# Reversing copies in eight parts, silu in single pieces and a weight gradient by column halves

## The chip, the core and the metric

The kernel runs on one core of one Trainium2 chip. The metric is the device time of one execution in microseconds (us). The core has a matrix engine (TensorE, PE in the profile; its weight loads are shown as PEld), a vector engine (VectorE, DVE), an engine for activation functions and copies (ScalarE, ACT), a general engine (GpSimd, POOL) and a queue engine (SyncE, SP). SP, ACT and POOL issue DMA transfers. Each engine takes its own instructions in a fixed order; semaphores join the engines.

## The reference

The program computes the output of a block and all its gradients. Of 2048 tokens and 576 channels, `A_u` is normalized; a state-space convolution `s` (a kernel from 128 complex rates for each channel, applied over the sequence) is gated by a feed-forward network with 4608 hidden columns.

```python
def _B_ref(x, w1, w3, w2):
    gate = jnp.einsum("bsd,df->bsf", x, w1)
    up = jnp.einsum("bsd,df->bsf", x, w3)
    h = _silu(gate) * up
    out = jnp.einsum("bsf,fd->bsd", h, w2)
    return out
...
    xn = _layernorm(x, axis=-1)
    s = _A_ref(xn, A_A_re, A_A_im, A_B_re, A_B_im, A_C_re, A_C_im, A_log_dt, A_Dskip)
    g = _silu(_B_ref(xn, B_w1, B_w3, B_w2))
    return x + s * g
...
    _out, _vjp = jax.vjp(_f, A_u, A_A_re, A_A_im, A_B_re, A_B_im, A_C_re, A_C_im, A_log_dt, A_Dskip, B_w1, B_w3, B_w2)
    _grads = _vjp(grad_out)
    _out0 = jnp.asarray(_out)
    return (_out0, *[jnp.asarray(_g) for _g in _grads])
```

`out_0` is the output, `out_1` the gradient of `A_u`, `out_2` to `out_9` those of the convolution's parameters, and `out_10`, `out_11` and `out_12` those of `w1`, `w3` and `w2`.

## The kernel before

The 2048 tokens are 16 tiles of 128 rows. The odd tiles are handled with their rows reversed, since the Fourier transforms work with sums and differences of mirrored rows. So `A_u` and `grad_out` are copied in DRAM, with the rows of each odd tile reversed, to a scratch tensor `odd`, and `out_0` and `out_1` are written for the odd tiles to `odd` and then copied back, reversed. The function `turned` gives the view of the eight odd tiles with their rows in reverse. A row has 1152 bytes, a whole copy 1152 KB.

The stages, in order of time. (1) Normalization, the state-space kernel and the gate and up products of the network (`ffn_hidden`, 72 steps of two tiles by 512 hidden columns). POOL stores the gate and up values (`G_dram`, `U_dram`), SP the hidden values. (2) `ffn_output`: w2's product for each tile, the output, and `go_o`, the gradient at the network's output. (3) The gradient groups: 18 groups of 256 hidden columns, with the gradient of the convolution in four quarters beside groups 0 to 10, and the sums for the state-space parameters (`param_step`) from group 11 on. (4) `phase6_inputs`: the gradient of `A_u`, tile by tile, odd tiles first, with the rest of the parameter sums beside it.

One gradient group `gi` runs through these stages (`phase6_group`, `phase6_grad13`). In "h0" to "h3" PE multiplies the output gradient with w2 into PSUM tiles `ph` (line 1746, 20 matmuls of 256 columns for a stage), ACT copies them to `gh` (line 1749), and DVE multiplies `gh` into the prepared tiles `gu` and `gg` (line 1764). "stored" is the store of both to DRAM on SP. Then come nine blocks of weight gradients: four 128-row blocks for `out_11`, four for `out_10` (line 1807, 16 matmuls each, copied by ACT at line 1809) and a tail of 32 matmuls for the last 64 rows of both (lines 1817 and 1819). They use two PSUM buffers, `pgw`, in turn. w2's own gradient (`phase6_grad2`, line 1787, 32 matmuls of 288 columns for 128 hidden columns) is called at "h1" and "h3" and takes both buffers at once, one for each half of the 576 output columns; ACT copies them at line 1791.

`phase6_prep` prepares the next group: silu of the gate values into `gu` (line 1713), the derivative of silu into `gg` (line 1717), and on DVE the products of both with the up values (lines 1720 and 1721). It is a generator; the loop in `backward` calls `next(prep)` at chosen stages, and each call emits the work up to the next `yield`. Each of silu and its derivative is done in four quarters of the tokens, in two calls of two quarters. The calls are at "h2" and "h3" for silu, at the first two blocks of `out_11` for the derivative, and at the next four blocks for one quarter of the products each.

What sets the order: `issue_after` puts an instruction behind another on its engine, and `self.sc` chains the ACT copies and activations of the groups in the order in which the program emits them. `self.at` gives a planned time; a planner orders what isn't chained by these times and by when inputs are ready.

The reversing copies before: `grad_out` in one copy on ACT's queue during the state-space kernel (line 569); `out_0` in one copy on SP at the start of the gradient groups (line 1200); `out_1` in two copies of four tiles each on POOL (line 1934), emitted at the 11th and 14th tile of the last stage and issued by the planner as soon as their inputs are stored.

## Time and profile before

| | |
|---|---|
| median of 3 runs | 1788.87 us (1781.19 to 1794.86) |
| the profiled execution | 1793.5 us |
| its span | 1791.7 us |
| granted clock of TensorE, mean | 0.988 |
| HBM read and written | 135.60 and 190.89 MB |

The span is the time from the first instruction to the last; the page divides it among the engines. A row of the waits names the instruction that stood still, what released it, the total time, the number of times and the longest. A row of a timeline gives start and duration in us, engine, line, what is written and read, how many instructions are merged, and in square brackets how long the engine was idle before and what ended that. SPq is the sequencer of SP, which issues transfers in order. A row of the groups gives the number of instructions, their busy time in us, the mean of one in ns, and the idle time before them.

### The profile page before, as it was taken

What the parts mean: (1) busy time and instruction counts of PE and PEld (TensorE: products, weight loads), DVE (VectorE), ACT (ScalarE), POOL (GpSimd) and SP (SyncE); (2) the same over time, 40 slices, a digit from 0 to 9 for tenths busy, and PEclk for the clock granted to TensorE, in tenths of its full rate; (3) what the DMA queues carried; (4) which work ended last, traced back from release to release, by engine and by line L of the source; (5) the groups of instructions that cost most, each with busy time, mean ns of one, the idle gap of its engine ahead of it and who ended that gap; (6) DMA issues with size and microseconds to landing.
All of it is one profiled execution on the core that took longest, in us unless ns stands there. A gap on an engine that the chain in (4) does not pass through costs nothing. (4 is left out here: it accounts for less than half of the span.)

```text
span 1791.7 us, 38769 instructions
## 1 busy us (share of the span) xinstructions
PE 1664.5 (93%) x15637; PEld 1228.2 (69%) x15637; DVE 1358.6 (76%) x2102; ACT 912.5 (51%) x1649; POOL 347.1 (19%) x565
## 2 busy tenths in 40 slices
PE   7789999999999999989999999999999987989997
PEld 3455555554545777777888888888888765768875
DVE  8768888887692555858978889659999955858675
ACT  6778888886864112764666666564445410101001
POOL 3112222213134111101111111111111233131032
PEclk9999999999999999999999999999999999999999
DMA  7789999889698989748666756589999999999992
GB/s 225 266 271 343 321 343 316 297 271 275 212 294 245 233 195 196 219 145 238 190 179 206 202 174 191 158 221 275 247 262 241 220 232 235 211 212 225 233 240 48
DMA packets 635483, 416.90 MB, mean 233 GB/s; under 512 B 424407, under 2 KB 575943, under 8 KB 630695
## 3 DMA queue, kind: packets, MB, share of 16 engines
q1 hardware_dynamic: 579620, 287.34, 64.5%
q0 software_dynamic: 31904, 106.81, 18.2%
q10 hardware_dynamic: 23778, 20.28, 4.2%
q8 instruction: 122, 2.00, 0.5%
q14 instruction: 59, 0.48, 0.1%
HBM read 135.60 MB, written 190.89 MB: 182 GB/s over the span
## 5 line engine op out<-in xcount | busy, mean ns | idle before, releaser
L1857 PEld LDWEIGHTS <-acts 128*128 128x128 bf16 x2304 | 224.9, 98 | 75.2 <-DMA acts<-GU_dram 11.4
L1807 PEld LDWEIGHTS <-xn_bf 128*128 128x128 bf16 x2304 | 224.5, 98 | 44.6 <-issue 18.4
L1394 DVE TENSOR_TENSOR pr_q<-et_ps,pz 128x1024 f32<-128x1024 f32 x144 | 176.0, 1222 | 29.5 <-PE et_ps L1389 14.8
L1857 PE MATMUL px<-wT,acts 128*128 128x288 bf16 x1472 | 191.6, 288 | 1.5 <-DMA wT<-in_B_w_dram 1.5
L1746 PE MATMUL ph<-w2T,goT 128*128 128x256 bf16 x1440 | 176.2, 275 | 8.7 <-ACT gh L1749 8.5
L1025 PEld LDWEIGHTS <-xnT 128*128 128x128 bf16 x1152 | 107.0, 98 | 109.2 <-issue 18.3
L1397 DVE TENSOR_REDUCE S_all<-pr_q 128x32 f32<-128x1024 f32 x144 | 175.3, 1217 | 3.1
L1746 PEld LDWEIGHTS <-goT 128*128 128x128 bf16 x1440 | 140.4, 99 | 28.8 <-issue 11.4
L1025 PE MATMUL pg<-wmB_w,xnT 128*128 128x512 bf16 x576 | 154.0, 380 | 2.1 <-ACT g_t L1041 1.8
L1025 PE MATMUL pu<-wmB_w,xnT 128*128 128x512 bf16 x576 | 154.3, 379 | 0.0
L1787 PE MATMUL pgw<-go_o,h_n 128*128 128x288 bf16 x1152 | 149.0, 286 | 0.2
L1807 PE MATMUL pgw<-gu_n,xn_bf 128*128 128x256 bf16 x1152 | 135.2, 273 | 10.4 <-ACT gw L1791 5.5
L1787 PEld LDWEIGHTS <-h_n 128*128 128x128 bf16 x1152 | 112.3, 98 | 30.0 <-issue 2.0
L1807 PE MATMUL pgw<-gg_n,xn_bf 128*128 128x256 bf16 x1152 | 130.5, 272 | 2.4 <-ACT gw L1809 2.3
L1809 ACT CAST gw<-pgw 128x256 bf16<-128x256 f32 x144 | 52.3, 374 | 144.6 <-PE pgw L1807 144.5
L1039 ACT ACTIVATE s_t<-pg 128x512 bf16<-128x512 f32 x144 | 87.8, 610 | 74.0 <-PE pu L1033 36.2
L1857 PE MATMUL px<-wA,acts 128*128 128x288 bf16 x832 | 110.5, 288 | 15.7 <-DMA acts<-GU_dram 10.5
L674 ACT ACTIVATE cs_k<-et_ps 128x512 bf16<-128x512 int16 x216 | 111.5, 630 | 0.1
L1749 ACT CAST gh<-ph 128x512 bf16<-128x512 f32 x144 | 81.3, 600 | 54.9 <-PE ph L1746 54.9
L1913 ACT ACTIVATE go<-gx 128x576 bf16<-128x576 f32 x16 | 10.9, 684 | 193.1 <-DVE gx L1896 109.4
L1053 POOL DMA_DIRECT2D G_dram<-g_t x72 | 52.4, 727 | 285.0 <-DVE g_t L1043 146.4
L1044 ACT CAST u_t<-pu 128x512 bf16<-128x512 f32 x144 | 87.4, 607 | 7.6 <-PE pu L1025 7.5
(316 smaller groups left out, 3206.0 us busy)
## 6 DMA issues: line engine op xcount, KB each, us to landing
U_dram<-u_t POOLq DMA_DIRECT2D x72, 256.0 KB, 5.3
G_dram<-g_t POOLq DMA_DIRECT2D x72, 256.0 KB, 4.7
H_dram<-h_t SPq DMA_DIRECT2D x72, 256.0 KB, 4.0
Q_dram<-q_k SPq DMA_DIRECT2D x36, 512.0 KB, 4.7
gg_n<-G_dram POOLq DMA_DIRECT2D x18, 1024.0 KB, 6.7
h_n<-U_dram POOLq DMA_DIRECT2D x18, 1024.0 KB, 8.6
GU_dram<-gu_n SPq DMA_DIRECT2D x36, 512.0 KB, 4.3
GG_dram<-gg_n SPq DMA_DIRECT2D x36, 512.0 KB, 10.5
```

The lines of the kernel that those rows point to most:

```text
L674: self.sin_last = nc.scalar.activation(out=CS[:, :, o:o + 256], in_=pt[:].bitcast(I16)[:, :, 0::2], func=ACT.Sin, scale=6.283184 / 2 ** 16)
L1025: ins = nc.tensor.matmul(pt[:], lhsT=xnT[:, c, ts], rhs=wm[w][:, c, :], start=(q == 0 and c == 0), stop=(q == 1 and c == nfull - 1))
L1039: nc.scalar.activation(out=s_t[:, :, q, :], in_=pgv, func=ACT.Silu)
L1044: nc.scalar.copy(out=u_t[:, :, q, :], in_=puv)
L1053: self.u_stores[step] = nc.gpsimd.dma_start(out=dst[fb * ng:(fb + 1) * ng, :, i0:i0 + NT, :].rearrange("g p t f -> p g (t f)"), in_=src[:] ...
L1394: nc.vector.tensor_tensor(out=pr[:].rearrange("p r k e -> p r (k e)"), in0=T[h][:].rearrange("p k z d a -> p (k z d a)")[:, None].to_broad ...
L1397: nc.vector.tensor_reduce(out=self.S_all[:, :, d0:d0 + 4], in_=pr[:].rearrange("p r k (d a) -> p (r k) d a", d=4), op=ALU.add, axis=AX.X)
L1746: self.pe_last = nc.tensor.matmul(ph[j][:, k, :].rearrange("p (a f) -> p a f", f=P), lhsT=lw, rhs=rh, start=(n == 0), stop=(n == nfull))
L1749: self.sc(lambda: nc.scalar.copy(out=gh[:, j], in_=ph[j][:]))
L1787: self.pe_last = nc.tensor.matmul(pgw[pi_][:, 0:pw], lhsT=hn[:, tt, fl * P:(fl + 1) * P], rhs=go_o[:, tt, po:po + pw], start=(tt == 0), st ...
L1807: self.pe_last = nc.tensor.matmul(pw_[:, 0:FG], lhsT=self.xn_bf[:, tt, c * P:(c + 1) * P], rhs=nat[:, tt, :], start=(tt == 0), stop=(tt == ...
L1857: self.pe_last = nc.tensor.matmul(px[pi_][:, 0:pw], lhsT=acts[i][:, ai, fi, :], rhs=w[:, po:po + pw], start=(n == 0), stop=(n == len(steps ...
```

## The change

1. `grad_out`: instead of one copy on ACT's queue, eight pieces of 16 row positions of each odd tile on POOL's queue, each behind the store of a step (36 to 50, every second one) of `ffn_hidden`.
2. `out_0`: instead of one copy on SP, eight pieces on SP, one in each of groups 2 to 9, behind the group's last store to `GG_dram` (`turn_out`).
3. `out_1`: instead of two copies of four whole odd tiles, eight pieces of 16 row positions of all eight odd tiles on POOL, two emitted at each of the 11th to 14th tile.
4. `phase6_prep`: eight calls with one quarter of silu or of its derivative each. The products of a quarter are emitted a call after its derivative, those of the last two quarters together. The calls move from "h2", "h3", four blocks of `out_11` and two of `out_10` to "h3", four blocks of `out_11` and three of `out_10`. For group 0, outside of the loop, all eight calls come before the convolution's last opening step.
5. `phase6_grad2`: the 16 matmuls of the first column half run before the 16 of the second; before, they took turns.

```diff
+    def turn_out(self, k):
+        sl = slice(16 * k, 16 * k + 16)
+        with self.tc.issue_after(self.gg_store.ins):
+            self.nc.sync.dma_start(out=self.turned(self.aps["out_0"].flatten_outer_dims())[:, sl],
+                                   in_=self.odd["out_0"][:, sl])
...
-            with self.tc.issue_after(self.sin_last.ins):
-                nc.scalar.dma_start(out=self.odd["grad_out"][:], in_=self.turned(self.aps["grad_out"].flatten_outer_dims()))
+            pass
...
+                if 36 <= step < 52 and step % 2 == 0:
+                    sl = slice(8 * step - 288, 8 * step - 272)
+                    with self.tc.issue_after(self.u_stores[step].ins):
+                        nc.gpsimd.dma_start(out=self.odd["grad_out"][:, sl],
+                                            in_=self.turned(self.aps["grad_out"].flatten_outer_dims())[:, sl])
...
-            self.at(T0 + 60)
-            nc.sync.dma_start(out=self.turned(self.aps["out_0"].flatten_outer_dims()), in_=self.odd["out_0"][:])
...
             with self.tc.issue_after(self.sgos[cfg.LT - 2].ins):
                 next(prep)
+                next(prep)
+            next(prep)
             next(prep)
...
             next(group)
             next(prep)
+            next(prep)
             next(group)
             with self.tc.issue_after(self.dft_copy.ins):
+                next(prep)
                 next(prep)
...
-                    if stage in ("h2", "h3", "out_11_0", "out_11_1", "out_11_2", "out_11_3", "out_10_0", "out_10_1"):
+                    if stage == "h3" or stage[:-1] in ("out_11_", "out_10_") and stage != "out_10_3":
                         next(prep, None)
...
+                    if stage == "out_11_2" and 0 <= gi - 2 < 8:
+                        self.turn_out(gi - 2)
...
-        halves = (quarters[0:2], quarters[2:4])
-        for part in halves:
-            for sl in part:
-                self.sc(lambda: nc.scalar.activation(out=gu[:, sl, :], in_=gg[:, sl, :], func=ACT.Silu))
-            yield
-        for part in halves:
-            for sl in part:
-                self.sc(lambda: nc.scalar.activation(out=gg[:, sl, :], in_=gg[:, sl, :], func=ACT.Derivative_silu))
-            yield
-        for sl in quarters:
+
+        def products(sl):
             nc.vector.tensor_tensor(out=gg[:, sl, :], in0=gg[:, sl, :], in1=hn[:, sl, :], op=ALU.mult)
             nc.vector.tensor_tensor(out=hn[:, sl, :], in0=gu[:, sl, :], in1=hn[:, sl, :], op=ALU.mult)
+
+        for sl in quarters:
+            self.sc(lambda: nc.scalar.activation(out=gu[:, sl, :], in_=gg[:, sl, :], func=ACT.Silu))
+            yield
+        for s, sl in enumerate(quarters):
+            self.sc(lambda: nc.scalar.activation(out=gg[:, sl, :], in_=gg[:, sl, :], func=ACT.Derivative_silu))
+            if s:
+                products(quarters[s - 1])
+            if s == 3:
+                products(sl)
             yield
...
-            for tt in range(LT):
-                for pi_, (po, pw) in enumerate(pieces):
+            for pi_, (po, pw) in enumerate(pieces):
+                for tt in range(LT):
...
-        if i in (10, 13):
-            q = slice(0, 4) if i == 10 else slice(4, 8)
-            self.nc.gpsimd.dma_start(out=self.turned(self.aps["out_1"].flatten_outer_dims(), q.start, q.stop), in_=self.odd["out_1"][q])
+        if i in (10, 11, 12, 13):
+            for k in range(2 * i - 20, 2 * i - 18):
+                sl = slice(16 * k, 16 * k + 16)
+                self.nc.gpsimd.dma_start(out=self.turned(self.aps["out_1"].flatten_outer_dims())[:, sl],
+                                         in_=self.odd["out_1"][:, sl])
```

More of the change, by code (lines that the diff above doesn't have):

```diff
@@ L1768, in phase6_group @@
                 ts = slice(j * LH, (j + 1) * LH)
-                self.sp(lambda: nc.sync.dma_start(out=dst[ts, :, gi * FG:(gi + 1) * FG].rearrange("t p f -> p t f"),
-                                                  in_=t_[:, ts, :]))
+                self.gg_store = self.sp(lambda: nc.sync.dma_start(
+                    out=dst[ts, :, gi * FG:(gi + 1) * FG].rearrange("t p f -> p t f"), in_=t_[:, ts, :]))
         yield "stored"
```

## The prediction

> **What bounds the kernel now.** I read the page's busy shares first, then the table of PE's waits, then tables by stage, then the timelines of the two longest stalls.
>
> ```profile
> span 1791.7 us, 38769 instructions
> PE 1664.5 (93%) x15637; PEld 1228.2 (69%) x15637; DVE 1358.6 (76%) x2102; ACT 912.5 (51%) x1649; POOL 347.1 (19%) x565
> ```
>
> PE, the matrix engine, is busy 93% of the span. The profiled execution took 1793.5 us, 1.8 more than its span; the median of the three runs is 1788.87, 4.6 lower. I subtract the gains from the median. A change pays where PE stands still, and this is what it stands still for (total, times, longest):
>
> ```profile
> PE px L1857 <- DMA acts<-GU_dram: 10.5, 3, 7.2
> PE ph L1746 <- ACT gh L1749: 8.5, 5, 5.3
> PE et_ps L1389 <- DMA gz<-gK_dram: 7.4, 2, 6.6
> PE pgw L1807 <- ACT gw L1809: 6.7, 18, 1.2
> PE pgw L1807 <- ACT gw L1791: 5.5, 11, 0.7
> ```
>
> The first line belongs to the loads that open the last stage, and the change does not touch them. The other four, 28.1 us, are what it can reach: ScalarE (ACT) late with a copy out of PSUM, and one late load. Two stretches of the gradient groups (start:end, length, busy us of PE, weight loads, DVE, ACT, POOL) show where a saved wait counts:
>
> ```profile
> 738.00:1206.00 468.00, 439.70 (x4372) 379.59 (x4371) 365.31 (x664) 290.35 (x516) 54.54 (x91) 0.99 0.66 190
> 1239.10:1390.30 151.20, 143.88 (x1403) 123.32 (x1402) 148.78 (x160) 75.81 (x123) 19.21 (x32) 1.00 1.03 251
> ```
>
> In groups 1 to 11 (the first row) VectorE (DVE) is busy 78% and PE decides. In groups 12 to 16 DVE is busy 148.78 of 151.20 us: there DVE decides, and a wait taken from PE comes back as a wait for DVE. So of the ACT waits only those of the first row count:
>
> ```profile
> PE et_ps L851 <- DVE Z L875: 6.7, 5, 3.8
> PE pgw L1807 <- ACT gw L1809: 5.4, 12, 1.2
> PE pgw L1807 <- ACT gw L1791: 3.5, 6, 0.7
> ```
>
> **The change: silu in single pieces.** Rows with busy us and mean ns:
>
> ```profile
> L1713 ACT ACTIVATE gu_n<-gg_n 128x1024 bf16<-128x1024 bf16 x72 | 72.3, 1054 | 0.2
> L1713 ACT ACT_TABLE_LOAD x18 | 23.1, 1283 | 0.7 <-DMA gg_n<-G_dram 0.4
> L1809 ACT CAST gw<-pgw 128x256 bf16<-128x256 f32 x144 | 52.3, 374 | 144.6 <-PE pgw L1807 144.5
> 801.94 7.15 PE L1807 MATMUL pgw<-gg_n,xn_bf 128*128 128x256 bf16 x64
> ```
>
> A block of a weight gradient is 16 matmuls, 16 x 7.15/64 = 1.79 us, in one of two PSUM buffers, so its copy must be done within two blocks, 3.58 us, of the copy before. Now two pieces, and in a first pair the table load, go ahead of a copy: 1.283 + 2 x 1.054 + 0.374 = 3.77 us, and the second pair follows at once. With one piece it is 1.283 + 1.054 + 0.374 = 2.71 us at most, and 1.43 without the load. The pieces (72 and 72) and table loads (18 and 18) are as many as before, so ACT does no more. The 5.4 us should go.
>
> The copy of the fourth hidden-gradient tile also stood behind a pair of silus. This is the longest gap that ACT makes:
>
> ```profile
> 785.35 1.43 ACT L1340 ACTIVATE gk_st<-et_ps,lcol 128x144 bf16<-128x144 f32 x2
> 786.79 1.28 ACT L1713 ACT_TABLE_LOAD   x1
> 788.09 2.00 ACT L1713 ACTIVATE gu_n<-gg_n 128x1024 bf16<-128x1024 bf16 x2
> 790.00 1.05 ACT L1749 CAST gh<-ph 128x512 bf16<-128x512 f32 x2
> 790.61 2.72 PE L1746 MATMUL ph<-w2T,goT 128*128 128x256 bf16 x12 [5.31 <-ACT gh L1749]
> ```
>
> With no piece at "h2" the copy can follow line 1340 at once: 790.00 - 786.79 = 3.2 us earlier. The 2.1 us behind line 1340 may stay. After the gap PE ran slowly, 12 matmuls in 2.72 us where the rate above gives 1.34; of these 1.4 I take half. Gain 3.9, between 0 (another wait appears, as the Z wait of 3.8 that is next on PE) and 6.7 (5.31 + 1.4).
>
> **w2's gradient by halves.** Both accumulators ended together and ACT copied one after the other, so the next block waited (3.5 us in the first row's stretch). Now the first half ends 16 matmuls before the second. Its weight tile is loaded twice either way:
>
> ```profile
> L1787 PEld LDWEIGHTS <-h_n 128*128 128x128 bf16 x1152 | 112.3, 98 | 30.0 <-issue 2.0
> L1787 PE MATMUL pgw<-go_o,h_n 128*128 128x288 bf16 x1152 | 149.0, 286 | 0.2
> ```
>
> There is one load for each matmul now, so the new order adds none. In group 0, where the products come in quarters while PE works, half as many matmuls are ready per quarter; I put +1.0 on that (8 matmuls, 8 x 0.12). Its products also move ahead of the convolution's first DVE instructions there, 8 x 0.685 = 5.5 us (the row is below) that must run at this place anyway: 0, at worst 5.5.
>
> Of 5.4 + 3.5 = 8.9 us I take half, 4.5: the Z wait (6.7) shows that PE, arriving sooner, meets DVE. Bounds 0 and 8.9.
>
> **The products later.** In the loop they move two or three stages on, the last four behind the last derivative at "out_10_2".
>
> ```profile
> L1720 DVE TENSOR_TENSOR gg_n<-gg_n,h_n 128x1024 bf16<-128x1024 bf16 x72 | 48.4, 685 | 31.8 <-ACT gg_n L1717 31.8
> L1394 DVE TENSOR_TENSOR pr_q<-et_ps,pz 128x1024 f32<-128x1024 f32 x144 | 176.0, 1222 | 29.5 <-PE et_ps L1389 14.8 <-DMA pz<-PZ_dram 6.6
> L1397 DVE TENSOR_REDUCE S_all<-pr_q 128x32 f32<-128x1024 f32 x144 | 175.3, 1217 | 3.1
> ```
>
> From the end of that stage PE still has a block, the tail (32 matmuls) and three hidden-gradient stages (60) before it needs the first multiplied tile's buffer: 108 x 0.112 = 12.1 us. The last piece and four products take 1.05 + 4 x 0.685 = 3.8. The slack of 8.3 us covers one parameter step (2 x (1.222 + 1.217) = 4.9), not two. Queued behind the late products on DVE are that step and the next group's multiplications, and PE waits for both. Cost 0; without the slack 2.7 us a group.
>
> **The row-reversing copies.** out_1's first half went out in the tail:
>
> ```profile
> 1553.07 1.18 POOL L1934 DMA_DIRECT2D out_dram<-odd_out  x1 [4.45 <-DMA odd_out<-go]
> 1551.08 8.73 SPq L1669 DMA_TRANSPOSE acts<-GU_dram  x1
> 1559.90 10.55 SPq L1669 DMA_TRANSPOSE qT<-Q_dram  x1
> 1574.99 1.01 PE L1389 MATMUL et_ps<-gz,qT 128*128 128x128 bf16 x8 [6.61 <-DMA gz<-gK_dram]
> 1575.79 4.43 PE L1857 MATMUL px<-wT,acts 128*128 128x288 bf16 x20
> 1738.51 10.29 PE px L1857 x84
> DMA to landing us min/median/max: 12.2/15.0/17.9
> ```
>
> The copy is issued at 1553.07 and lands 17.9 us later (the last line, of both halves). Meanwhile SP's queue, which issues in order, is held 10.55 us on one transposing load; gz is issued behind it, and PE waits 6.61 us. The next 20 matmuls take 4.43 us instead of 20 x 10.29/84 = 2.45. Together 8.6 us. Each new piece takes rows of all eight odd tiles, so none can start before the last odd tile is stored, where the second half starts now:
>
> ```profile
> 1636.00 4.99 SPq L1669 DMA_TRANSPOSE acts<-GU_dram  x1
> 1645.70 12.74 SPq L1669 DMA_TRANSPOSE acts<-GG_dram  x1
> 1600.00:1700.00 100.00, 100.00 (x875) 81.17 (x874) 70.58 (x79) 9.28 (x18) 11.59 (x17) 1.00 1.16 225
> odd_A_u<-in_A_u_dram POOLq DMA_DIRECT2D x1, 1152.0 KB, 11.2
> ```
>
> There the half copy stretched a load by 12.74 - 4.99 = 7.75 us, yet PE was busy all of 1600 to 1700: loads run far enough ahead. Twice the bytes now come at this place. A copy of all eight blocks, like the last row's, took 11.2 us for twice the bytes of a half, less than either half's 12.2 or 17.9; so I take the burden as unchanged there, and the 8.6 us as gained.
>
> The Trainium skill (DMA: Bandwidth & Descriptors, "Why a DMA increments its semaphore by 16 and not by 1") says that a copy runs on the largest number of engines up to 16 that divides the slowest dimension of both patterns. By that rule, the trace agrees: a half has 4 blocks, the whole 8, and the half is the slower.
>
> On POOL the eight issues cost between 0.53 us each (the first row below, of small stores) and 1.18 (row 1553.07, of four times the rows); the layer-norm operations queued behind them have an engine that is 19% busy, and the wait for the last odd tile's landing stands there already. grad_out's copy leaves ACT's queue for POOL's, and out_0's pieces go behind the GG stores of groups 2 to 9 on SP:
>
> ```profile
> L1483 POOL DMA_DIRECT2D out_dram<-WO_b x40 | 21.0, 531 | 34.4 <-DVE WO_b L1478 31.1 <-DMA out_dram<-WO_b 3.0 <-DVE S_all L1397 0.2
> L569 ACTq DMA_DIRECT2D odd_grad_out<-in_grad_out_dram x1: 775/775/775, 186.7 to 186.7; - x1
> L1200 SPq DMA_DIRECT2D out_dram<-odd_out x1: 762/762/762, 730.1 to 730.1; - x1
> ```
>
> PE's waits show no load late behind either, so no gain; eight issues of 0.76 us at most are 6.1 us of a queue each, hidden by loads that run ahead. If not hidden, 12 us are lost. I take 0.
>
> **Sum.** -8.6 - 3.9 - 4.5 + 1.0 = -16.0: 1788.9 - 16.0 = 1772.9, say 1773. Its own range, from half to one and a half of the gain, is 1765 to 1781.
>
> **The rivals.** *The tail stall only moves.* Twice the bytes stretch the loads at 1645 by up to 7.75 us more, the lead is used up, and the 8.6 us return: 1773 + 8.6 = 1782. For it: the SP queue is in steady use there. Against it: PE at 100.00 with the half. The skill's same page ("Rules for kernel authors") advises merging small transfers because each carries a fixed cost; at its 2.0 us, six more pieces would, if nothing overlapped, make 12 us, an estimate that gives 1785.
>
> *Everything counts.* All 28.1 us of reachable waits and the slow matmuls (1.4 + 2.0) go, less what DVE holds in groups 12 to 16: about 27 us, 1762. For it: group 1's stores leave earlier, so the Z wait may shrink too. Against it: DVE's 98%.
>
> *The products come too late.* If two parameter steps or the convolution's products stand before them on DVE, the slack of 8.3 us is gone and each of 17 group changes waits for four products, 2.74 us: 46.6 us, so 1773 + 47 = 1820; with half of them 1796. It decides from a DVE backlog of 8.3 us. For it: groups 12 to 16 have no DVE reserve. Against it: between two steps PE itself needs several us.
>
> *The order does not come out as written.* The planner reorders instructions that are ready; then nothing moves much: 1789.
>
> **Chances.** Forecast 0.57, tail moves 0.13, everything counts 0.15, products late 0.11, reordered 0.04. About 1% (17.9 us) is what a measurement of this kernel can tell from no change. Faster by more means below 1771: the third case and nearly half of the forecast's (0.27), 0.42. Slower by over 1%, above 1807, needs most of the late products: with their milder half counted at the border, 0.09. The rest, 0.49, is within 1%. The range 1753 to 1797 holds all but the worse half of the late products and the ends of the others.
>
> **What would show it.** Right: no load on SP near a reversing copy held for 10 us before the last odd tile; no PE wait for gz of 6 us; PE's waits of line 1807 for lines 1791 and 1809 nearly gone in groups 1 to 11; the gap at 790 at 2 us. Wrong: PE waiting for acts or gz behind the eight pieces (the first rival), PE waiting at ph for gh behind DVE's line 1764 (the third), or DVE's waits in groups 1 to 11 growing by what ACT's shrink.

## The result, and the profile after

The changed kernel took 1786.63 us (median of 20 runs, 1770.99 to 1802.88) where the kernel before took 1802.68 (20 runs, 1781.19 to 1826.84): a ratio of 0.9939, 95% interval 0.9912 to 0.9966. Two more sets of runs of the same kernel gave 0.9872 (0.9815 to 0.9929) and 0.9899 (0.9864 to 0.9933). Weighted by their intervals the three make 0.992, that is 0.8% faster. Ratios, and means over profiles, leave out slow executions (over 1.5% above the fastest of their kernel), and two of the profiled ones are slow: out_1 alone (1804.6 us) and prep and halves (1830.6 us).

The forecast time was 1773, between 1765 and 1781, and the measured 1786.63 lies above that. Its base, 1788.87, was the median of only three runs of the kernel before; that of twenty is 13.8 us higher. As a ratio the forecast was 1772.9 / 1788.9 = 0.991, and its range, 0.987 to 0.996, holds all three.

The page of the profiled execution (1785.93 us, span 1784.1), its first lines:

```profile
span 1784.1 us, 38717 instructions
PE 1657.9 (93%) x15573; PEld 1230.5 (69%) x15637; DVE 1357.9 (76%) x2102; ACT 919.2 (52%) x1649; POOL 352.6 (20%) x579
```

The busy times are those of before within 7 us each. What PE stood still for (total, times, longest):

```profile
PE et_ps L1397 <- DMA gz<-gK_dram: 17.1, 5, 7.4
...
PE pgw L1823 <- ACT gw L1807: 7.3, 15, 2.0
...
PE et_ps L856 <- DVE Z L880: 6.7, 4, 4.9
PE px L1873 <- DMA acts<-GU_dram: 6.5, 1, 6.5
...
PE ph L1762 <- ACT gh L1765: 3.1, 4, 1.6
...
PE pgw L1823 <- ACT gw L1825: 1.2, 2, 0.7
```

Line 1823 is line 1807 of before, 1825 its 1809, 1807 its 1791, 1762 its 1746, 1397 its 1389 and 856 its 851. The copies of weight gradients (1825) now hold PE for 1.2 us instead of 6.7, the hidden-gradient copies for 3.1 instead of 8.5, as forecast; those of w2's gradient (1807), which the halves were to shrink, rose from 5.5 to 7.3. And gz rose from 7.4 to 17.1, and Z, although both gaps at the start of the groups are gone, still stands at 6.7 with a new longest wait of 4.9. Groups 1 to 11 and 12 to 16 by windows, columns as before:

```profile
740.80:1210.60 469.80, 440.05 (x4386) 380.59 (x4385) 365.50 (x663) 293.35 (x516) 54.41 (x91) 0.99 0.69 189
1242.80:1400.10 157.30, 143.87 (x1382) 122.67 (x1381) 146.56 (x158) 76.74 (x123) 18.87 (x32) 0.98 1.04 241
```

Groups 1 to 11 took 469.8 us against 468.0 before. Up to group 9 this execution is about 10 us ahead (the first ruler below), and groups 10 and 11 lose it again. Part of that loss is a slow stretch of DMA. SP's timeline and the PE row behind it:

```profile
1159.76 5.54 SPq L1683 DMA_TRANSPOSE qT<-Q_dram  x1
1165.40 2.25 SPq L1384 DMA_DIRECT2D gz<-gK_dram  x2
1167.75 17.94 SPq L1785 DMA_DIRECT2D GG_dram<-gg_n  x2
```

```profile
1189.69 1.01 PE L1397 MATMUL et_ps<-gz,qT 128*128 128x128 bf16 x8 [7.35 <-DMA gz<-gK_dram]
```

The issue of a store is held 17.94 us, and PE waits 7.35 us for a gz whose issue was done at 1167.65. A second execution of the same kernel ("again" below) had no wait of PE over 2 us between 1000 and 1230.

### The profile page after: what moved, and what is told of

It reads as the page before. It is cut to its first block, busy times and chain, and to the rows that moved or that the text cites. A ratio compares the mean times of both kernels' runs of the same rounds, so it can differ in the third digit from the quotient of the medians.

```text
span 1784.1 us, 38717 instructions
## 1 busy us (share of the span) xinstructions
PE 1657.9 (93%) x15573; PEld 1230.5 (69%) x15637; DVE 1357.9 (76%) x2102; ACT 919.2 (52%) x1649; POOL 352.6 (20%) x579
## 5 line engine op out<-in xcount | busy, mean ns | idle before, releaser
L1873 PE MATMUL px<-wT,acts 128*128 128x288 bf16 x1472 | 189.3, 286 | 0.0
L1030 PE MATMUL pg<-wmB_w,xnT 128*128 128x512 bf16 x526 | 143.6, 379 | 10.4 <-issue 5.6
L1803 PE MATMUL pgw<-go_o,h_n 128*128 128x288 bf16 x1152 | 153.0, 288 | 0.2 <-DVE h_n L1727 0.2
L1873 PE MATMUL px<-wA,acts 128*128 128x288 bf16 x832 | 111.5, 292 | 10.7 <-DMA acts<-GU_dram 6.5
L1726 DVE TENSOR_TENSOR gg_n<-gg_n,h_n 128x1024 bf16<-128x1024 bf16 x72 | 48.8, 683 | 59.3 <-ACT gg_n L1733 57.1
L1808 POOL DMA_DIRECT2D out_dram<-gw x36 | 19.9, 552 | 362.3 <-ACT gw L1807 191.3
```

The source lines that it names most:

```text
L1030: ins = nc.tensor.matmul(pt[:], lhsT=xnT[:, c, ts], rhs=wm[w][:, c, :], start=(q == 0 and c == 0), stop=(q == 1 and c == nfull - 1))
L1726: nc.vector.tensor_tensor(out=gg[:, sl, :], in0=gg[:, sl, :], in1=hn[:, sl, :], op=ALU.mult)
L1803: self.pe_last = nc.tensor.matmul(pgw[pi_][:, 0:pw], lhsT=hn[:, tt, fl * P:(fl + 1) * P], rhs=go_o[:, tt, po:po + pw], start=(tt == 0), st ...
L1873: self.pe_last = nc.tensor.matmul(px[pi_][:, 0:pw], lhsT=acts[i][:, ai, fi, :], rhs=w[:, po:po + pw], start=(n == 0), stop=(n == len(steps ...
```

## The experiments

"Copies" are edits 1 to 3 of the change; the "group part" is edit 4 (the pieces of silu and its derivative with the products, "prep") and 5 (w2's gradient by halves). Two stretches of each profile are used as rulers. *Groups 0 to 9* runs from the last store to `GS_dram` to group 9's first store to `GU_dram`. *Tail* runs from the first px matmul of the sixth token tile to that of the sixteenth, which holds the stall at 1575 of before and the second half of out_1's copies. SP's rows that bound the first, for the kernel before:

```profile
722.61 0.37 SPq L1145 DMA_DIRECT2D GS_dram<-gs_t  x1
...
1128.25 1.02 SPq L1769 DMA_DIRECT2D GU_dram<-gu_n  x2
```

| kernel | ratio to before, 95% interval | groups 0 to 9, us | tail, us |
|---|---|---|---|
| before | 1 | 405.6 | 199.0 |
| whole change, three sets | 0.9939, 0.9872, 0.9899 | 395.8, 397.5, 397.0 | 187.7, 195.4, 189.3 |
| out_1's pieces alone | 0.9965 (0.9917 to 1.0012) | 405.4 | 200.3 |
| grad_out's pieces alone | 0.9968 (0.9932 to 1.0004) | 405.6 | 194.9 |
| out_0's pieces alone | 0.9941 (0.9911 to 0.9971) | 395.0 | 209.3 |
| out_0 whole, at group 2 | 1.0001 (0.9971 to 1.0031) | 402.0 | 196.3 |
| grad_out's and out_0's pieces | 0.9896 (0.9834 to 0.9958) | 395.1 | 187.8 |
| all three copies | 0.9942 (0.9902 to 0.9982) | 394.9 | 200.7 |
| all three, and halves | 0.9902 (0.9870 to 0.9934) | 394.2 | 189.5 |
| prep alone | 0.9984 (0.9949 to 1.0018) | 404.3 | 205.2 |
| halves alone | 1.0003 (0.9969 to 1.0036) | 404.6 | 195.5 |
| prep and halves | 1.0090 (1.0050 to 1.0130) | 410.3 | 187.9 |
| prep, variant copy behind | 0.9976 (0.9933 to 1.0018) | 400.6 | 202.3 |
| prep and halves, variant copy behind | 0.9977 (0.9935 to 1.0019) | 399.7 | 194.5 |
| whole change, one stage earlier | 0.9985 (0.9954 to 1.0016) | 398.0 | 187.5 |
| whole change, variant copy behind | 0.9938 (0.9896 to 0.9979) | 390.6 | 193.9 |
| grad_out whole, on POOL | 1.0032 (0.9991 to 1.0073) | 405.1 | 187.7 |
| grad_out in seven pieces | one run, 1778.95 us | 405.0 | 186.9 |

The first ruler repeats within 2 us between kernels that share the edits which act there. The whole time scatters by over 1%, the tail by 8 us between three executions of the whole change and by 22 between kernels with out_1's copies as before. So most of what follows is read from the first ruler, and the ratio says how much of it was left at the end.

### The change once more, its three parts

The whole change was run again; then out_1's copies alone, the group part alone, and the copies of grad_out and out_0 alone (each is the change cut to those hunks; their first lines are shown):

The whole change again:

> The changed kernel once more, nothing edited. In its first profile the transposing load of qT issued at 1159.8 landed 28.7 us later, with 8192-byte packets of up to 7.5 us, and PE then waited 7.35 us for gz in group 10. If the new order of the loads makes that slow stretch (theory A), it stands in this profile too, with a landing over 20 us at the first qT load and PE waiting for gz for 5 us or more in groups 10 to 16, and the time is again 0.4 to 0.9% below before. If it was an accident of that execution (theory B), this profile has no landing of qT over 15 us there and a span some 10 us shorter.

out_1 alone:

```diff
-        if i in (10, 13):
...
+        if i in (10, 11, 12, 13):
+            for k in range(2 * i - 20, 2 * i - 18):
...
```

> Only out_1's copies in eight pieces; all else as before. By the prediction PE's wait of 6.6 us for gz near 1575 and the slow matmuls behind it go: 8.6 us, 0.5% faster (0.3 to 0.6%). If the tail stall only moves, the time is within 0.1% of before and PE waits for acts or gz between 1640 and 1700.

The group part alone:

```diff
-        for part in halves:
...
+        for sl in quarters:
...
-            for tt in range(LT):
-                for pi_, (po, pw) in enumerate(pieces):
+            for pi_, (po, pw) in enumerate(pieces):
+                for tt in range(LT):
```

> Only the gradient groups' part: silu and its derivative in single pieces, products later, w2's gradient by halves; all copies as before. By the prediction 3.9 + 4.5 - 1.0 = 7.4 us, 0.4% faster, and PE's waits for line 1749 and for the copies of weight gradients nearly gone in groups 1 to 11. If the new order of the loads slows the start of the parameter sums (theory A), groups 10 to 16 give 10 us or more back, PE waits there for gz, and the time is within 0.3% of before.

grad_out and out_0 alone:

```diff
+                if 36 <= step < 52 and step % 2 == 0:
...
-            nc.sync.dma_start(out=self.turned(self.aps["out_0"].flatten_outer_dims()), in_=self.odd["out_0"][:])
...
+                    if stage == "out_11_2" and 0 <= gi - 2 < 8:
+                        self.turn_out(gi - 2)
```

> Only grad_out's and out_0's copies in pieces and in their new places; all else as before. By the prediction nothing: within 0.2% of before. If the pieces on SP behind the GG stores cost what they could (eight issues), up to 0.4% slower.

The slow stretch at 1160 to 1190 did not come back in the second execution of the whole change, whose span is 11.4 us shorter; so it does not belong to the order of loads, as theory B has it. The surprise was in the parts: the two moves whose terms were nothing made the kernel 1% faster, and the group part, whose terms were -3.9, -4.5 and +1.0, made it 0.9% slower. By group 9 it has already lost 4.7 us, where theory A, which looks to groups 10 to 16, has no loss.

### out_0's copy: the order that it makes

out_0's pieces alone, edit 2 of the change; then out_0's copy whole, only moved behind group 2's last store, which differs from the first so:

```diff
-                    if stage == "out_11_2" and 0 <= gi - 2 < 8:
-                        self.turn_out(gi - 2)
+                    if stage == "out_11_2" and gi == 2:
+                        with self.tc.issue_after(self.gg_store.ins):
+                            nc.sync.dma_start(out=self.turned(self.aps["out_0"].flatten_outer_dims()), in_=self.odd["out_0"][:])
```

> Only out_0's copy is changed: it leaves SP's queue at 730 and goes as eight pieces behind the GG stores of groups 2 to 9. Theory A (the whole gain of the two moves comes from the copy's old place: with it there, w2T's loads follow group 0's stores and the KH loads follow group 1's, and PE waits 5.31 at 790 and 3.79 at 816): group 2's GU store comes about 10 us earlier than before, the gaps at 790 and 816 are gone, and the time is that of both moves together, ratio about 0.990. Theory B (grad_out's pieces on POOL carry it): no difference from before, ratio 1.00, and both gaps still there. Nothing is left out of the computation.

> out_0's copy is kept whole, 1152 KB in one transfer on SP, and only moved behind the GG store of group 2. Theory A (its place matters, not the parts): the gaps at 790 and 816 are gone as with the pieces, group 2's GU store about 10 us earlier than before, ratio about 0.990, within 0.4% of the run with the pieces. Theory C (the parts matter: a whole transfer of 1152 KB in the groups holds the loads of the next convolution quarter): a new wait of PE for Z, gz or ph of 4 us or more behind the copy, in the 25 us after it is issued, and a ratio of 0.995 or more.

The pieces alone shorten the first ruler by 10.6 us, and every kernel with them and without the group part has 394.9 to 395.1. Both gaps of before, 5.31 at 790 and 3.79 at 816, are gone, although silu, its derivative and the gradient copies were not touched. SP's timeline of before from the old copy on:

```profile
730.14 0.76 SPq L1200 DMA_DIRECT2D out_dram<-odd_out  x1
739.60 1.02 SPq L1769 DMA_DIRECT2D GU_dram<-gu_n  x2
740.71 3.61 SPq L1769 DMA_DIRECT2D GG_dram<-gg_n  x2
744.42 5.72 SPq L1669 DMA_TRANSPOSE w2T<-w2r  x2
...
797.88 5.80 SPq L86 DMA_DIRECT2D a<-KH_dram  x1
```

and of out_0's pieces alone:

```profile
735.37 2.81 SPq L1675 DMA_TRANSPOSE w2T<-w2r  x2
...
743.28 3.66 SPq L1775 DMA_DIRECT2D GU_dram<-gu_n  x2
...
769.71 0.34 SPq L86 DMA_DIRECT2D a<-KH_dram  x1
```

Without the copy, w2's weights are loaded 9.0 us earlier, ahead of the stores, and the convolution's `a` 28.2 us earlier. The engines' order from there on is another; PE's rows of the same kernel, under the same pair of silus, show it:

```profile
775.89 4.53 PE L1752 MATMUL ph<-w2T,goT 128*128 128x256 bf16 x40
780.26 4.08 PE L1793 MATMUL pgw<-go_o,h_n 128*128 128x288 bf16 x32
```

ACT's rows there:

```profile
778.88 1.28 ACT L1719 ACT_TABLE_LOAD   x1
780.18 2.00 ACT L1719 ACTIVATE gu_n<-gg_n 128x1024 bf16<-128x1024 bf16 x2
782.09 1.05 ACT L1755 CAST gh<-ph 128x512 bf16<-128x512 f32 x2
```

The copy of gh waits behind a table load and a pair of silus as before, 3.2 us. But PE has w2's gradient, 32 matmuls and 4.08 us, to do meanwhile. Before, it had ten matmuls there and then nothing:

```profile
784.05 1.25 PE L1746 MATMUL ph<-w2T,goT 128*128 128x256 bf16 x10
```

So at this place what PE had to do meanwhile decided, and not how long the copy was held up. That the earlier loads made this order is read from the rows; no run moved the loads alone.

The whole copy at group 2 shows where theory A ends. Its loads are as early as with the pieces (w2T at 733.0, `a` at 767.4) and the same gaps are gone: group 3's GU store comes 14.5 us earlier than before. The copy is issued at 835, and by group 9 only 3.6 us are left; PE waits 1.56 us for ph at 898, 3.18 us for Z at 951 and 1.54 us for ph at 994. The ratio is 1.000, as theory C has it, but the wait of 4 us within 25 us behind the copy, theory C's sign, is not there. Taking the copy away from its old place makes the gain; with the copy whole at group 2 most of it is lost again. Whether its size does that, or the order that came with this place, these runs do not separate.

### The group part: prep alone, halves alone

> Only the silu and derivative pieces and the products are moved to the new stages; w2's gradient keeps its order and all reversing copies stay. Theory A (the pieces change the order in which the planner puts DVE's copies of the convolution ahead of its Z work, and PE then waits for Z and ZZ): waits for Z and ZZ of 3 us or more in three or more places between 840 and 1130, ACT's waits at line 1807 shrunk from 6.7 to under 2, ratio 1.005 to 1.010. Theory B (the loss of the two group edits together comes from w2's gradient by halves): ratio 0.995 to 1.000.

> Only w2's gradient goes by column halves. Theory A (the pieces make the loss): PE's wait of line 1807 for line 1791's copies shrinks from 5.5 to under 3, nothing else moves by more than 2 us, ratio 0.997 to 1.001. Theory B (the halves make it): ratio 1.005 to 1.010, with new waits for Z or ZZ in groups 1 to 11.

The edits are the two hunks of the diff, each by itself. Halves alone did nothing (1.0003; PE's waits for line 1791's copies in groups 1 to 11 went from 3.5 to 3.9 us, not below 3 as theory A had it). ACT's and PE's rows at one of these waits, halves alone, show why:

```profile
876.44 2.01 ACT L1713 ACTIVATE gu_n<-gg_n 128x1024 bf16<-128x1024 bf16 x2
878.35 0.70 ACT L1791 CAST gw<-pgw 128x288 bf16<-128x288 f32 x2
```

```profile
873.62 4.08 PE L1787 MATMUL pgw<-go_o,h_n 128*128 128x288 bf16 x32
878.79 3.43 PE L1807 MATMUL pgw<-gu_n,xn_bf 128*128 128x256 bf16 x30 [0.55 <-ACT gw L1791]
```

The first half is complete after 16 of the 32 matmuls, near 875.7, but ACT's order has a pair of silus in front of both copies, and it makes them one behind the other at 878.35, as before.

Prep alone also took away the gap at 790 (group 2's GU store 14.2 us earlier than before), and this with out_0's copy still in its place and the loads as late as before (w2T at 747.3, `a` at 794.2): the copies of gh now come ahead of the silus, as forecast, and a wait of 2.01 us for line 1791's copies (1797 here) is left at 789. But by group 9 all but 1.3 us was given back, in three waits of 5.33, 4.02 and 4.60 us for Z and ZZ. DVE's rows ahead of the first:

```profile
834.67 0.45 DVE L876 TENSOR_TENSOR Z<-Z,cm_t 128x576 bf16<-128x576 bf16 x1
839.11 0.31 DVE L857 COPY a<-a 128x576 bf16<-128x576 bf16 x1 [3.99 <-DMA a<-UH_dram]
839.34 0.68 DVE L1716 TENSOR_TENSOR gg_n<-gg_n,h_n 128x1024 bf16<-128x1024 bf16 x1
...
845.86 0.45 DVE L876 TENSOR_TENSOR Z<-Z,cm_t 128x576 bf16<-128x576 bf16 x1
```

and PE's:

```profile
845.99 1.24 PE L851 MATMUL et_ps<-Z,cT 128*128 128x144 bf16 x9 [5.33 <-DVE Z L875]
```

DVE stands 3.99 us at a copy for the next quarter of the convolution, whose load has not landed; behind it in DVE's order are the eight products (0.68 us each, the first is shown) and the last Z operations of the present quarter, which wait for nothing. Prep and halves together are slower than the two alone would add up to, 410.3 us on the first ruler at the same granted clock there as before, 0.98: they have such waits at 851, 900, 955 and 1117.

### Earlier stages, and the copy put behind

Is it that the products come too late, or where that copy stands? First the whole change with every call one stage earlier:

```diff
-                    if stage == "h3" or stage[:-1] in ("out_11_", "out_10_") and stage != "out_10_3":
+                    if stage in ("h2", "h3") or stage[:-1] in ("out_11_", "out_10_") and stage not in ("out_10_2", "out_10_3"):
```

> The whole change, with each silu, derivative and product one stage earlier in the loop (from the third hidden-gradient stage on, as the pairs were). Theory A (the products come too late on DVE and so stand between the convolution's loads and its Z work): the wait for Z of 5 us at 940 that both profiles of the whole change have is gone or under 2 us, ACT's waits for line 1807 stay as small as with the whole change (under 3 us in groups 1 to 11), and the ratio is 0.3 to 0.5% below the whole change's: 0.983 to 0.990. Theory B (the wait at 940 comes from the planner's new order whatever the stage): it is still there, or as long elsewhere, and the ratio is the whole change's.

The wait for Z was still there (5.39 us at 944): one stage of lateness does not make it, and theory A falls. The ratio, 0.9985, is not the whole change's either, as theory B had it; its profile has a wait of 10.53 us for gz at 1298, and what made it is open. Then the copy of a quarter's first variant was tied behind the last multiply-accumulate of the quarter before, in three kernels, with the whole change run once more beside them:

```diff
-                with self.tc.issue_after(self.cm_last.ins) if b else nullcontext():
+                with self.tc.issue_after(self.cm_last.ins):
                     self.spectrum_variants(A2[b], Az[b])
```

> The whole change, and each convolution quarter's first variant copy on DVE (a from a, which waits for that quarter's load) ordered behind the quarter before it's last multiply-accumulate, as the later copies already are. Theory A (the wait for Z at 940 comes from that copy, which the planner puts in front of the last nine Z operations on DVE once the silu pieces have moved): the wait of 4.9 to 5.7 us there is gone or under 1.5 us, group 6's GU store comes about 5 us earlier against group 3's than with the whole change, and the time is 0.2 to 0.4% below the whole change of the same set. Theory B (DVE is behind at that place whatever the order): the wait is still 3 us or more, or as long at the next group, and the time is the whole change's.

> The two group edits alone (silu pieces and products at the new stages, w2's gradient by halves), and the first variant copy ordered behind the last Z operation as above. Theory A: the waits for Z of 5.1 at 851 and 5.2 at 955, which the two edits alone showed, are gone or under 1.5 us; the ratio falls from 1.009 to 0.996 to 1.001, since the gain at 790 now stays. Theory B: the waits come back elsewhere in groups 2 to 8 and the ratio stays over 1.004.

> Only the silu pieces and products at the new stages, and the first variant copy behind the last Z operation. Theory A: the wait for Z of 5.3 at 846 is gone, the waits for ZZ of 4.0 at 896 and 4.6 at 1106 stay, since there DVE waits for another load (az) with the products queued behind it; group 3's GU store about 5 us earlier than with the pieces alone, ratio 0.993 to 0.997. Theory B: ratio that of the pieces alone, 0.998.

> The changed kernel once more, beside the three above on the same chip. Theory A: the wait for Z at 940 is there again with 4.9 to 5.7 us, and no wait for gz of 3 us or more between 1550 and 1590; ratio 0.987 to 0.994. Theory B (the wait at 940 was chance in two profiles): it is absent.

DVE and PE of the whole change, in this last run of it:

```profile
928.25 0.45 DVE L881 TENSOR_TENSOR Z<-Z,cm_t 128x576 bf16<-128x576 bf16 x1
932.71 0.31 DVE L862 COPY a<-a 128x576 bf16<-128x576 bf16 x1 [4.01 <-DMA a<-UH_dram]
...
941.93 0.45 DVE L881 TENSOR_TENSOR Z<-Z,cm_t 128x576 bf16<-128x576 bf16 x1
```

```profile
942.07 2.08 PE L856 MATMUL et_ps<-Z,cT 128*128 128x144 bf16 x16 [5.00 <-DVE Z L880]
```

and with the copy behind:

```profile
938.86 0.45 DVE L881 TENSOR_TENSOR Z<-Z,cm_t 128x576 bf16<-128x576 bf16 x1
939.22 0.68 DVE L1780 TENSOR_TENSOR gg_n<-gh,gg_n 128x1024 bf16<-128x1024 bf16 x1
939.83 0.30 DVE L862 COPY a<-a 128x576 bf16<-128x576 bf16 x1
```

```profile
938.99 1.16 PE L856 MATMUL et_ps<-Z,cT 128*128 128x144 bf16 x16 [0.91 <-DVE Z L880]
```

The copy now waits for nothing and PE 0.91 instead of 5.00 us; PE's 16 matmuls after the long wait took 2.08 us, after the short one 1.16. At this place the copy's position in DVE's order is shown to make the wait: one constraint was added and the wait went. On the first ruler the whole change goes from 395.8, 397.5 and 397.0 to 390.6, prep and halves from 410.3 to 399.7, prep from 404.3 to 400.6 (its waits for ZZ stay with 4.5 and 4.8 us, where another load is late, as expected). The ratio of prep and halves falls from 1.009 to 0.998, as expected; that of prep, 0.9976 against 0.9984, is theory B's. Theory A holds for these waits. For the whole change the total did not follow: 0.9938 with the copy behind and 0.9899 without, in the same set. The 5 to 7 us are 0.3 to 0.4%, no more than the intervals; and the profile with the copy behind has new waits further on, 7.30 us at 1250 and 5.19 us at 1589, both for DVE's parameter sums.

### All three copies without the group part

Against the whole change, first without edits 4 and 5, then without edit 4 alone:

```diff
-                    if stage == "h3" or stage[:-1] in ("out_11_", "out_10_") and stage != "out_10_3":
+                    if stage in ("h2", "h3", "out_11_0", "out_11_1", "out_11_2", "out_11_3", "out_10_0", "out_10_1"):
...
-            for pi_, (po, pw) in enumerate(pieces):
-                for tt in range(LT):
+            for tt in range(LT):
+                for pi_, (po, pw) in enumerate(pieces):
```

> The whole change without its group part: grad_out's, out_0's and out_1's copies in pieces, the silu and derivative pieces, the products and w2's gradient as before. Theory A (the gain is in out_0's and out_1's copies, and the group part gives its own gain back as waits for Z): no wait of PE over 2 us between 780 and 1430, no wait for gz over 3 us between 1550 and 1590, and faster than the whole change, whose ratio was 0.987 and 0.994 in two sets of runs: 0.984 to 0.990. Theory B (the group part still saves what its ACT waits showed, about 5 us): slower than the whole change, 0.992 to 0.996.

> The three copies in pieces and w2's gradient by column halves, the silu pieces and products as before. Theory A (the halves alone change nothing but their own wait): PE's waits behind line 1791's copies fall below 3 us in all, no new wait for Z, ratio within 0.2% of the run without the halves. Theory B (the halves pull the group and the convolution against each other): new waits for Z or ZZ of 3 us in groups 1 to 11 and a ratio at least 0.4% higher.

On the first ruler theory A has it in both: no wait over 2 us in groups 0 to 9, 394.9 and 394.2 us. Its other sign fails: PE's waits behind w2's copies are 3.2 us in groups 1 to 11 and 5.3 in all, with the halves as without. By the ratios, 0.9942 and 0.9902, the first lies in theory B's band and the second is lower by 0.4% than the first, with intervals that overlap and a tail of 200.7 against 189.5 us in their profiles. They do not tell these kernels from the whole change, and none of the versions run beats it by more than the intervals.

### grad_out's copy

```diff
-            with self.tc.issue_after(self.sin_last.ins):
-                nc.scalar.dma_start(out=self.odd["grad_out"][:], in_=self.turned(self.aps["grad_out"].flatten_outer_dims()))
+            pass
...
+                if step == 36:
+                    sl = slice(0, 128)
```

> Only grad_out's copy is changed: from ACT's queue to eight pieces on POOL's. Theory A (it is hidden either way): group 0's GU store within 2 us of before, the gaps of before at 790 and 816 still there, ratio 0.997 to 1.003. Theory B (it carries the difference between both moves, 0.990, and out_0's alone, 0.994): ratio 0.994 to 0.997, with the first sweep shorter by 5 us or more.

> grad_out's copy on POOL's queue as one transfer instead of eight pieces; all else as before. All eight kernels without grad_out's pieces whose POOL issues number 493 end with a drain on POOL of 10.3 us, the one with 499 with 10.8 us; those with 501 and 507 with 2.2 and 2.6 us, and a span that ends 3.3 to 4.1 us sooner after the last token tile begins. Theory A (the length of POOL's last drain depends on how many transfers POOL has issued): 494 issues give 10.3 to 10.4 us, the last stretch is 29.7 us as before, ratio 1.000 within 0.3%. Theory B (taking the copy off ACT's queue shortens it): drain about 2.2 us and last stretch 26.4 us, as with the eight pieces.

> grad_out's copy on POOL's queue in seven pieces, the last of double size: 500 issues of POOL. Theory A: the drain is either 10.9 us (the count still below the turn) or 2.1 us (at or past it), since it grows by about 0.08 us an issue on both sides; nothing else differs from the run with eight pieces. Theory B: 2.2 us, as with eight pieces.

The first is the hunk of the change; the lines above are for one transfer on POOL, and seven pieces are the eight with the last two joined. In its own stage the move by pieces is hidden (group 0's GU store 2.9 us later than before, first ruler 405.6). The gain is at the very end. The last transfer that ACT issues in the kernel before (span 1791.7) and with grad_out's eight pieces (span 1787.2):

```profile
1784.86 0.34 ACTq L1931 DMA_DIRECT2D out_dram<-go  x1
```

```profile
1783.62 0.34 ACTq L1935 DMA_DIRECT2D out_dram<-go  x1
```

From there to the end are 6.8 us before and 3.6 us with the pieces. The last long drain instruction on POOL takes 10.3 us before and ends 0.8 us ahead of the kernel's end; with eight pieces it takes 2.2 us and ends 2.6 us ahead. In all nine kernels with grad_out's copy on ACT's queue it takes 10.3 or 10.8 us; in the whole change 2.6, with seven pieces 2.2. As one transfer it took 3.6 us, and the stretch from the last token tile on 25.7 us instead of 29.7: theory A falls (494 transfers there, 493 before), and theory B has the direction. What sets the length is open, and so is whether leaving ACT's queue or joining POOL's does it: no run puts the copy on a third. The profile with one transfer on POOL also has a wait for V of 13.76 us at 409 in the first sweep, which ends 18 us later at its last store, and the ratio is 1.0032 (0.9991 to 1.0073): here too the whole transfer comes with a wait that the pieces do not have.

## Why the prediction was right or wrong

**The sum** was -16.0 us, 0.9%; measured 0.6, 1.3 and 1.0%, weighted 0.8%. That the size came out is luck; as a time it missed, since its base was too low. By the rulers out_0's move, put at 0, gave 10.6 us, and grad_out's, put at 0, 3 to 4; the group part, put at -7.4, cost 1.8 on top of out_0's move; and the tail, put at -8.6, was about 4 shorter. An unpriced gain stood in for terms that failed.

**The step that failed: out_0's move at 0.** Its eight issues were priced as queue time, "hidden by loads that run ahead", while the loads behind the old copy on SP, w2's and the convolution's, were not looked at. They are 9.0 and 28.2 us earlier without the copy, and groups 0 to 9 are 10.6 us shorter.

**The tail (-8.6), right in kind, too large.** The wait for gz around 1550 to 1590 recurs: of eleven profiles with out_1's copies in whole halves eight have it, 2.5 to 7.3 us, as this one with out_0's pieces alone:

```profile
1560.59 1.01 PE L1393 MATMUL et_ps<-gz,qT 128*128 128x128 bf16 x8 [5.73 <-DMA gz<-gK_dram]
```

Of seven profiles with the pieces none has one of 2 us there, and in the changed kernel SP holds no load for 8 us between 1540 and the first piece. The load of qT at the place where one was held 10.55 us before:

```profile
1560.70 3.37 SPq L1683 DMA_TRANSPOSE qT<-Q_dram  x1
```

The wait goes with a slow first half: the eight halves with it land after 14.5 to 18.7 us, the other three after 10.7 to 11.7. Those three, and all seven with the pieces, also have grad_out's copy on POOL (and so has one of the eight, grad_out's pieces alone). With that copy on ACT only out_1 alone has the pieces; its profile has no such wait, but one of 2.35 us for gz at 1633, before its pieces go out. So the pieces' share is not separated from that of grad_out's move. The tail stretch is 196.3 us in the mean of the eleven and 192.0 in that of the seven, 4 us and not 8.6 (they scatter over 22 and 13 us), and out_1 alone measured -0.35%, with no change inside the interval. In place of gz comes DVE:

```profile
1588.73 0.58 PE L1397 MATMUL et_ps<-gz,qT 128*128 128x128 bf16 x4 [5.19 <-DVE pr_q L1402]
```

This is from the whole change with the variant copy behind; five other profiles with the pieces have such waits of 2.5 to 6.1 us between 1580 and 1610. Profiles with the halves have them too, later, near 1735 (3.19 us in the kernel before). The forecast asked what is late next for silu, and not here. **The first rival** (the stall only moves to 1640) did not occur: after the pieces no wait over 1.7 us for a load follows in any profile, while with the halves one of 9.04 us for gz follows the second half (prep alone, at 1655). POOL's timeline of the changed kernel, with the first three pieces, and the landing times of all eight:

```profile
1638.91 1.94 POOL L1951 DMA_DIRECT2D out_dram<-odd_out  x3 [5.09 <-issue]
```

```profile
DMA to landing us min/median/max: 4.2/7.0/8.1
```

Here the pieces landed after 4.2 to 8.1 us, in other profiles after up to 13.7; the halves before after 12.2 and 17.9. The Trainium skill (DMA: Bandwidth & Descriptors, "Rules for kernel authors") advises to merge many small transfers and says that under 64 KB one pays mostly overhead. The pieces have 144 KB, and the 12 us that the rival estimated for them do not show as a wait of PE.

**The gap at 790 (-3.9): the cause right, but not the only one.** It was put down to the pair of silus in front of the gh copy. Prep alone takes the pair away and the gap goes, with 2.01 us left where the forecast left 2.1. But in out_0's experiment the pair stays and the gap goes too, since PE has other work under it. So one gap had two cures, each with its own edit, and in the whole change the term could not come on top of out_0's gain.

**The PSUM copies in groups 1 to 11 (-4.5, the half of 8.9): one half right, the payment missed.** The copies of line 1809 behave as forecast: the waits for them fall from 5.4 to 1.2 us. Those of line 1791, which were to save 3.5, do not: they stand behind silus and not behind each other, and the waits go from 3.5 to 4.2. The forecast halved the sum because "PE, arriving sooner, meets DVE"; what PE met was DVE's order, a copy in front of it that waits for a load, and 4 to 5 us at a time. As written the group part costs 396.8 (mean of three) - 395.0 = 1.8 us on top of out_0's move. The group part and the constraint on the variant copy together are worth 395.0 - 390.6 = 4.4 on top of that move; out_0's move with the constraint alone was not run, so the group part's share of this is not shown.

**Halves (+1.0): not seen** (0.03%, interval from -0.3 to +0.4%). **The products (0), and the third rival.** They were not late for their own reader: in groups 1 to 11 of the changed kernel PE waits 1.3 us in all, at most 0.6 at a time, for line 1764's multiplications (1780 there), and one stage earlier did not help, so that rival's mechanism falls. It was near in one thing: the products did push into the convolution's work on DVE, in prep's profile 5.5 us between the landed load and the last Z. The rival asked who waits for the products, not who is behind them.

**grad_out (0): wrong by 3 to 4 us**, through a drain at the end that no view used in the forecast shows. **That everything counts** did not happen: the waits for Z, gz and DVE took over. **That the order does not come out as written**, given 0.04, is the nearest to what was found: not that nothing moves, but that edits moved the order of work which they do not name.

**Open.** Whether the gz waits of groups 12 to 16, up to 10.5 us in one profile and absent in others, are more frequent with the group part; why the whole time scatters by over 1% between executions of one kernel; how much of the tail's gain is out_1's and how much grad_out's; and the drain.

## What to carry to other kernels

Where a planner orders the engines, price an edit by what it lets forward or pushes back in each queue, as well as by its own time: taking one large copy out of its place in SP's queue was worth 10.6 us, and with it two loads and the work under PE's gap had moved. After an edit, look on the engine that releases the longest new wait for an instruction that itself waits for a DMA with ready work behind it; one ordering constraint took 4 us of wait away without touching any work. And measure a stage by a stretch between two fixed events: it told 2 us apart, where the intervals of the whole time reach 5 to 10 us to either side.

## What the runs showed of the hardware

- POOL's last long drain took 10.3 to 10.8 us in nine kernels and 2.2 to 3.6 us in those with grad_out's copy on POOL's queue instead of ACT's; from the start of the last token tile to the end, the latter took 25.7 to 26.5 us, the nine 29.7 to 30.2.
- After a wait of 5.00 us PE ran 16 matmuls in 2.08 us, and the granted clock was 0.50 from 942.0 to 946.0; after one of 0.91 us the same took 1.16 us at a granted clock of 1.00. So the longer wait cost 0.9 us more than itself in the next 16 matmuls alone. The Trainium skill (TensorE: Matmul & The Clock Gate, "HAM oscillation — how this bites in real kernels") has idle gaps of PE over some 3.4 us end in a halved clock; these two rows agree.
- A slow stretch of DMA did not repeat: a store's issue held 17.94 us and a gz wait of 7.35 us in one execution of the changed kernel, neither of them in the two others.
